# Routing attention and a serf layer: passes over constants on TensorE in the prologue, and another order of shifts, similarities and first loads

## The chip, the core and the metric

The kernel runs on one core of a Trainium2 chip. The metric is the device time of one execution in microseconds (us), as the median of a few runs. The core has a matrix engine, TensorE (PE in the profile; its weight loads are PEld), three engines for elementwise work, VectorE (DVE), ScalarE (ACT) and GpSimd (POOL), and SyncE (SP), whose queue issues nearly all DMA transfers here. Each engine works through its own instructions in order; semaphores make it wait for others.

## The reference

Two layers follow each other. The first is attention with routing: queries and keys are each assigned to the nearest of 16 centroids of their head, by a cosine, and a query sees only the keys of its own cluster.

```python
q_assign = argmax(einsum(q_n, c_n)); k_assign = argmax(einsum(k_n, c_n))   # 16 clusters
scores = q @ k.T / sqrt(64), -1e9 where q_assign != k_assign               # (4, 8, 768, 768)
attn_out = softmax(scores) @ v                                             # (4, 8, 768, 64)
x = attn_out as (3072, 512); h = x @ w_in                                  # w_in (512, 2048)
out = (h * erf(softplus(h))) @ w_out                                       # w_out (2048, 512)
```

There are 32 heads of 768 tokens with 64 features, in f32.

## The kernel before, in words

**The two stages.** The first stage computes attention for 16 pairs of heads (p = 0 to 15; the two heads, e = 0 and 1, lie on partitions 0 to 63 and 64 to 127) and writes x to DRAM. The second multiplies by w_in and w_out in blocks of a Strassen-like scheme; the change does not touch it. Beside the attention the kernel prepares 22 pieces of the weights (`fetch`, `size_and_rest`, `bounded`, `sign`, `shifted`, `summed`, lines 220 to 246: one load, three ScalarE, two DVE and one POOL instruction for each), two in every pair from pair 0 to pair 10.

**A pair's parts**, each a function (lines 281 to 485):

- `load_qk` (169) issues eight DMAs of 96 KB for q and k; `transposes` (281) turns them on DVE and then asks for the next pair's loads, since there is one staging tile for q and one for k.
- `similarities` (293) multiplies by the normalized centroids in f32 (the tile `turned` <- qT, ccT or more_out, ccT); `choose` (306) finds each token's cluster on DVE in four instructions: sims, mx, hot, hotT. `masks` (332) spreads that over the partitions with one matmul (<- hotT, pick) and a ScalarE instruction that writes qm or km. There are four such masks in a pair: q and k, two halves each.
- A step, `maxima_step` (349), estimates the largest score of each query from bf16 copies: four matmuls into `wide` and a reduction on DVE (nmx) over all of it. Twelve steps make a pair. After steps 5 and 11 a small reduction (`lowest`) collects half of the queries.
- `turn` (372) makes the row of shifts of one half out of `lowest`: three matmuls of 128 columns into `turned`, and two ScalarE copies of one row each into qm.
- `products` (392) multiplies k and q in f32; `scores` (405) adds the mask and the shift to the same PSUM tile, so it needs the turned row; `curve` (418) is the exponential on ScalarE (pr <- sc). `accumulate` (423) sums on POOL, `attend` (435) multiplies by v, `divide` (447) makes the reciprocal of the sum (two ScalarE instructions `inv`, two DVE instructions `den`), scales and stores x.

**Periods.** A pair's attention is done in six periods, i = 0 to 5; a period handles two of the pair's twelve units (half of the queries, one sixth of the keys). `period` (705) writes the order out by hand, and all engines keep it: a step, perhaps a mask, products of two units, perhaps similarities of the pair two ahead (i = 3), a second step, perhaps a turn (i = 2 and 5), scores, exponentials, some preparation of weights, and attend for the units of the period before. Steps run ahead: the table `ahead` (689 to 695) gives the slot of each, such that steps of a pair are done in the pair before, 7 slots ahead (6 for some); step 6 of pair 1 stands alone at the end of pair 0. `MASKS` and `FIRST_MASKS` (47, 48) say where the masks of the next pair stand.

**The prologue** (lines 175 to 279 and 794 to 849) normalizes the centroids (a square root by logarithm and exponential on ScalarE and two rounds of Newton on DVE), turns them, sets constants, loads and turns pair 0, finds its clusters, loads v and five pieces of weights, makes steps 0 to 5, the first turn, a mask, and step 6.

**Names in the profile.** Nearly every instruction is recorded by one helper, so nearly all have line L59; they are told apart by their tiles. `wide` and `sc` are PSUM tiles; `turned` is two PSUM tiles for everything small and for attend's sums. An f32 matmul is recorded as two.

Of the kernel before, what the change touches and what calls it, by code (L numbers as in the profile page):

```python
# [9 lines left out]
F32 = mybir.dt.float32  # L10
# [57 lines left out]
def kernel(  # L68
# [81 lines left out]
    def load(p, nm, src, pl):  # L150
        if p >= NPAIR:
            return
        b, h0 = heads(p)
        if nm == "v":
            t = pl.tile([P, NJ, 2, D], F32, name="in_v")
            for e in range(2):
                queues[0].dma_start(out=t[:, :, e], in_=src[b, h0 + e].rearrange("(j p) d -> p j d", p=P))
        else:

            t = pl.tile([P, NB, Q], F32, name="in_" + nm)  # L160
            for e in range(2):
                for g in range(D // Q):
                    queues[e].dma_start(
                        out=t[e * D + g * Q : e * D + (g + 1) * Q],
                        in_=src[b, h0 + e, :, g * Q : (g + 1) * Q].rearrange("(n t) d -> t n d", t=Q),
                    )
        pairs.setdefault(p, {})[nm] = t

    def load_qk(p):
        load(p, "q", q, stage)  # L170
        load(p, "k", k, stage)


    setup = prs[-1].rearrange("p e n -> p (e n)")
# [2 lines left out]

    load_qk(0)
    queues[1] = sy
    tc.keep_in_program_order(nc.scalar.preload_act_table_set("natural_log_exp_and_others"))  # L180

    make_identity(nc, ident)
# [60 lines left out]
    def summed(n):  # L243
        w, lo = w_steps[n][0].bitcast(I32), steps[n][1].bitcast(I32)
        ge.tensor_tensor(out=w, in0=w, in1=lo, op=ALU.add)
        if n in after_of:
            fetch(after_of[n])

    cn = setup[:, D : 3 * D].rearrange("p (e d) -> p e d", e=2)
    spare = iter(range(3 * D, HW))  # L250

    def scalar_tile():
        n = next(spare)
        return setup[:, n : n + 1]
# [6 lines left out]
    norm = scalar_tile()  # L261
    ae.activation(out=norm, in_=ss, func=ACT.Ln)
    ae.activation(out=norm, in_=norm, func=ACT.Exp, scale=0.5)
    for it in range(2):
        inv = scalar_tile()
        ve.reciprocal(out=inv, in_=norm)
        twice = scalar_tile()
        ve.scalar_tensor_tensor(
            out=twice, in0=ss, scalar=inv, in1=norm, op0=ALU.mult, op1=ALU.add
        )  # L270
        norm = scalar_tile()
        ve.tensor_scalar(
            out=norm, in0=twice, scalar1=0.5, scalar2=(1e-6 if it else 0.0),
            op0=ALU.mult, op1=ALU.add,
        )
    rden = scalar_tile()
    ve.reciprocal(out=rden, in_=norm)
    for e in range(2):
# [2 lines left out]
    def transposes(p, which="qk"):  # L281

        if p >= NPAIR:
            return
        st = pairs[p]
        for nm in which:
            st[nm + "T"] = rows[p % 3][nm]
            ve.transpose(out=st[nm + "T"], in_=st.pop(nm).rearrange("p n t -> p (n t)"))
        if "k" in which:
            st.update(lows[p % 2])  # L290
            load_qk(p + 1)

    def similarities(p):

        if p >= NPAIR:
            return
        st = pairs[p]
        st["psim"] = turned[1][:, 0:HW]
        for g in range(4):
            te.matmul(  # L300
                st["psim"][2 * C * g : 2 * C * (g + 1)], lhsT=ccT[:, p % HP],
                rhs=st["qk"[g // 2] + "T"][:, (g % 2) * HW : (g % 2 + 1) * HW],
                start=True, stop=True,
            )
# [378 lines left out]
    def run(work):  # L683
        for _ in work:
            pass

    ahead = [[] for _ in units]
    for n in range(NJ + 1, 2 * NJ * NPAIR):  # L690
        if n == 3 * NJ:
            continue
        slot = n - NJ - (n < 2 * NJ or n > 3 * NJ)
        if slot < len(units):
            ahead[slot].append(divmod(n, 2 * NJ))

    def step_ahead(slot):
        for which in ahead[slot]:
            maxima_step(*which)

    forms = sum((left_forms(ve, *w_in_parts(f, 2)) for f in range(0, HF, 2)), [])
    routing = [iter(())]
# [2 lines left out]
    def period(p, i):  # L705
# [7 lines left out]
                return masks(p + 1, *which, turned[0 if i in (0, 5) else 1])  # L713
            return lambda: None

        step_ahead(u)
        mask(0)()
        next(part[0], None)
        products(u)
        products(u + 1)  # L720
        mask(1)()
        if i == 3:
            similarities(p + 2)
            routing[0] = choose(p + 2)
            next(routing[0], None)
        elif (p, i) == (0, 1):
            similarities(1)
            routing[0] = choose(1)
            next(routing[0], None)
        step_ahead(u + 1)  # L730
        next(part[0], None)
        if i in (2, 5) or (p, i) == (1, 0):
            for which in turns:
                turn(*which)
            turns.clear()
        scores(u)
        scores(u + 1)
        later = mask(2)
        curve(u)
        later()  # L740
        curve(u + 1)
        if i == 0 and early(n1 - 1):
            shifted(n1 - 1)
        elif i == 1 and early(n1):
            size_and_rest(n1)
        elif i == 2 and early(n1):
            bounded(n1)
            sign(n1)
        elif i == 3:
            if early(n1):  # L750
                shifted(n1)
            if early(n2):
                size_and_rest(n2)
        elif i == 4 and early(n2):
            sign(n2)
        elif i == 5 and early(n2):
            bounded(n2)
        if n1 - (i == 0) >= N_EARLY and i in (0, 2, 3, 5) and forms:
            forms.pop(0)()
        if i == 0:  # L760
            transposes(*((p + 2, "q") if p else (1, "k")))
        elif i == 1:
            load(p + 1, "v", v, vp)
            if p == 0:
                run(routing[0])
                vectors(1, "q")
                vectors(1, "k")
        elif i == 2:
            transposes(p + 2, "k" if p else "qk")
        elif i == 3:  # L770
            next(routing[0], None)
        elif i == 4:
            vectors(p + 2, "k")
        elif i == 5:
            run(routing[0])
            vectors(p + 2, "q")
# [10 lines left out]
                part[0] = divide(u - 1)  # L787
                next(part[0])
        mask(3)()
        if (p, i) == (0, 5):  # L790
            maxima_step(1, NJ)


    pct = turned[0][:, 0:P]
    te.transpose(out=pct, in_=cn.rearrange("p e d -> p (e d)"), identity=ident)
    ve.memset(nbig, 0.0)
    for e in range(2):
        ve.memset(nbig[e * D : e * D + C], -BIG)
        ve.memset(nbig[e * D + SH : e * D + SH + 1], 1.0)
    for t in maxima:  # L800
        ve.memset(t, FLOOR)
    ve.memset(pick, 0.0)
    ve.tensor_copy(out=identb, in_=ident)
    ve.memset(minus, -1.0)
    ve.memset(alleps, S * EPS)
    for t in lowest:
        ge.memset(t, 0.0)
    st = pairs[0]
    st["qT"], st["kT"] = rows[0]["q"], rows[0]["k"]
    ve.transpose(out=st["qT"], in_=st.pop("q").rearrange("p n t -> p (n t)"))  # L810
# [4 lines left out]
        )  # L815
    ve.transpose(out=st["kT"], in_=st.pop("k").rearrange("p n t -> p (n t)"))
    st.update(lows[0])
    load_qk(1)
    similarities(0)
    vectors(0, "q")  # L820
    vectors(0, "k")
# [6 lines left out]
                )  # L828
    also = ps_s.tile([P, 2, 512], F32, name="sc", tag="s")
    products(0)  # L830
    run(choose(0))
    transposes(1, "q")
    copies = [
        masks(0, nm, half, bank)
        for nm, half, bank in (("q", 0, wide[:, 0]), ("k", 0, turned[0]), ("k", 1, turned[1]))
# [2 lines left out]
    for copy in copies[1:]:  # L838
        copy()
    load(0, "v", v, vp)  # L840
    for n in range(PLACES):
        fetch(n)
    queues[0] = queues[1] = nc.sync
    for i in range(NJ):
        maxima_step(0, i, also if i % 2 else wide)
    turn(0, 0)
    turns.clear()
    masks(0, "q", 1, turned[1])()
    maxima_step(0, NJ)
    for p in range(NPAIR):  # L850
        for i in range(HJ * 2):
            period(p, i)
# [115 lines left out]
```

## Time and profile before

| what | us |
|---|---|
| median of 3 runs (lowest, highest) | 1052.26 (1051.94, 1052.99) |
| the profiled execution | 1051.62 |
| its span, first to last instruction | 1049.9 |
| TensorE busy | 1023.1 |
| DVE busy | 706.8 |
| ScalarE busy | 514.5 |
| POOL busy | 337.7 |
| mean granted TensorE clock | 0.993 |

The span is 1.72 us shorter than the profiled execution. The first instruction after the start stands at 0.30 us, the first exponential at 28.38, products of pair 1 at 59.22, and the last matmuls of the attention near 465. A timeline's row gives start, duration, engine, operation, tiles written <- tiles read, shape, and how often it stands there in a row; a bracket at its end gives the engine's idle time before it and what ended that. Matmuls overlap, so the duration of a row of several is longer than what they add to the time; the starts of successive rows tell that.

### The profile page before, as it was taken

How to read it: one execution, taken by the hardware profiler on the slowest of the kernel's cores; microseconds unless marked ns; L12 is line 12 of the kernel's file. 1: busy time of each engine (PE TensorE's matmuls, PEld its weight loads, DVE VectorE, ACT ScalarE, POOL GpSimd, SP SyncE). 2: the span in 40 equal slices, each digit the busy share in tenths (PEclk: the TensorE clock that was granted, in tenths of full speed). 3: DMA queues.
4: the chain of work that ended last, by engine and by line, in shares of the span. 5: the costliest groups of instructions: out<-in, count | busy, mean ns of one | idle time of the engine just before them, and what ended most of it. 6: DMA issues, size and time to landing. Idle time of an engine off the chain costs nothing.

```text
span 1049.9 us, 15192 instructions
## 1 busy us (share of the span) xinstructions
PE 1023.1 (97%) x5793; PEld 708.3 (67%) x5793; DVE 706.8 (67%) x1307; ACT 514.5 (49%) x674; POOL 337.7 (32%) x229
## 2 busy tenths in 40 slices
PE   4899999999999999999999999999999999999998
PEld 1344444444444444448888888888888888888887
DVE  6667777777777777747976656476465656564754
ACT  2667777777777666547643250505143222415050
POOL 1566777777667666666230000000000000000000
PEclk8999999999999999999999999999999999999999
DMA  8344443433342321113200010001011000000001
GB/s 191 61 101 101 97 97 94 100 94 88 86 101 51 94 57 31 31 67 117 81 0 19 23 41 1 21 22 39 1 41 41 1 11 31 1 1 21 21 1 40
DMA packets 141496, 55.53 MB, mean 53 GB/s; under 512 B 127088, under 2 KB 131184, under 8 KB 141424
## 3 DMA queue, kind: packets, MB, share of 16 engines
q1 hardware_dynamic: 138288, 54.18, 20.1%
q8 instruction: 45, 0.74, 0.3%
q10 hardware_dynamic: 3136, 0.39, 0.2%
q14 instruction: 27, 0.22, 0.1%
HBM read 41.98 MB, written 12.58 MB: 52 GB/s over the span
## 4 chain that ended last, share of the span: by engine, by line
PE 90%; DVE 6%; ACT 2%; issue 1%; POOL 1%; ACTq 0%; DVEq 0%; POOLq 0%
PE bank L59 42%; PE turned L59 29%; PE sc L59 13%; PE wide L59 7%; DVE nmx L59 3%; DVE den L59 2%; ACT pr L59 1%; POOL more_out L59 1%; ACT inv L59 1%; ACT qm L59 0%; ACT x_own L59 0%; ACT w_in L59 0%; ACTq L59 0%; DVE pr L59 0%; ACT L180 0%
## 5 line engine op out<-in xcount | busy, mean ns | idle before, releaser
L59 POOL TENSOR_TENSOR more_out<-more_out,pr 128x768 f32<-128x768 f32 x128 | 215.8, 1686 | 99.7 <-ACT pr L59 94.6
L59 DVE TENSOR_REDUCE nmx<-wide 128x2 f32<-128x768 f32 x189 | 180.3, 954 | 84.9 <-PE wide L59 83.0
L59 ACT ACTIVATE pr<-sc 128x768 f32<-128x768 f32 x192 | 146.9, 810 | 67.2 <-PE sc L59 66.4
L59 PE MATMUL turned<-pr,in_v 128*64 128x386 f32 x768 | 145.4, 500 | 0.1
L59 DVE TENSOR_TENSOR g<-bank,g 128x256 f32<-128x256 f32 x222 | 89.5, 421 | 56.7 <-PE bank L59 46.4
L59 PE MATMUL bank<-x_own,w_in 128*128 128x256 f32 x424 | 104.4, 379 | 0.0
L59 PE MATMUL bank<-w_out,g 128*128 128x256 f32 x448 | 103.1, 379 | 0.0
L59 PE MATMUL sc<-qT,kT 64*128 64x384 f32 x528 | 101.3, 494 | 0.0
L59 PEld LDWEIGHTS bank<-w_out,g 128*128 128x128 f32 x448 | 85.1, 190 | 11.6
L59 PEld LDWEIGHTS turned<-pr,in_v 128*64 128x64 f32 x768 | 46.6, 136 | 67.8 <-issue 63.2
L59 PEld LDWEIGHTS bank<-x_own,w_in 128*128 128x128 f32 x424 | 80.4, 190 | 12.1 <-issue 1.2
L59 PEld LDWEIGHTS <-qv 64*128 64x128 bf16 x384 | 27.2, 94 | 87.8 <-issue 75.2
L59 ACT COPY g<-bank 128x256 f32<-128x256 f32 x28 | 10.4, 372 | 152.1 <-PE bank L59 148.5
L59 DVE TENSOR_TENSOR osb<-bank,osb 128x256 f32<-128x256 f32 x87 | 35.4, 420 | 72.9 <-ACT osb L59 25.4
L59 ACT ACT_TABLE_LOAD x48 | 61.6, 1283 | 45.7 <-DVE g L59 45.1
L59 POOL TENSOR_TENSOR more_out<-pr,pr 128x768 f32<-128x768 f32 x32 | 58.4, 1826 | 62.6 <-ACT pr L59 62.6
L59 PE MATMUL bank<-x_more,more_in 128*128 128x256 f32 x296 | 76.0, 379 | 0.0
L59 PE MATMUL wide<-kv,qv 64*128 64x384 bf16 x378 | 68.6, 333 | 6.3 <-DVE nmx L59 4.0
L59 PE MATMUL wide<-km,qm 64*128 64x384 bf16 x378 | 67.2, 329 | 2.7 <-ACT qm L59 2.7
L59 PEld LDWEIGHTS sc<-qT,kT 64*128 64x128 f32 x528 | 52.2, 189 | 25.0 <-ACT pr L59 6.0
L59 PE MATMUL bank<-more_out,g_more 128*128 128x256 f32 x272 | 64.3, 379 | 0.0
L59 DVE TENSOR_TENSOR g<-a_s,g 128x512 f32<-128x512 f32 x96 | 62.5, 688 | 1.4 <-ACT a_s L59 1.4
(153 smaller groups left out, 1688.3 us busy)
## 6 DMA issues: line engine op xcount, KB each, us to landing
x_own<-in_moe_w_in_dram SPq DMA_DIRECT2D x13, 512.0 KB, 4.1
in_v<-in_v_dram SPq DMA_DIRECT2D x32, 192.0 KB, 2.9
x_dram<-more_out SPq DMA_DIRECT2D x32, 192.0 KB, 2.5
x_own<-x_dram SPq DMA_DIRECT2D x6, 1024.0 KB, 5.2
out_dram<-osb SPq DMA_DIRECT2D x24, 256.0 KB, 2.0
in_q<-in_q_dram SPq DMA_DIRECT2D x62, 96.0 KB, 3.0
in_k<-in_k_dram SPq DMA_DIRECT2D x62, 96.0 KB, 2.6
g_more<-in_moe_w_out_dram SPq DMA_DIRECT2D x6, 512.0 KB, 3.5
```

Of the source, the lines that this page charges most:

```text
L59: ins = getattr(self.engine, name)(*args, **kw)
```

## The change

It does the following:

- Loads: q and k of pair 1 are loaded into x_more, a tile that is free then, right behind pair 0's; pair 2's loads take the place that pair 1's had. The fifth piece of weights, which goes to x_more, is asked for behind the prologue.
- The constants (nbig, maxima, pick, identb, minus, alleps, lowest) are set ahead of the centroids' work; one of the two rounds of Newton is left out.
- `warm` puts matmuls of constants on TensorE whose result nobody reads: 24 of 256 columns ahead of the centroids' turning, 6 of 384 behind it, 15 behind the first products, 3 after each of steps 0 to 5, and 2 before the first turn. Those of 384 columns read `lowest[0]`.
- The mask of q's second half comes after step 1, not after the turn; q of pair 1 is turned ahead of `choose(0)`, k of pair 1 in the prologue.
- Steps stand six slots ahead in every case, two in each period (in period 0 of pair 0 one, behind the exponentials).
- A turn stands first in periods 0 and 3, not between the second step and the scores of periods 5 and 2.
- Similarities stand behind the scores of their period, not ahead of its second step.

```diff
--- before.py
+++ after.py
@@ -157,7 +157,11 @@
                 queues[0].dma_start(out=t[:, :, e], in_=src[b, h0 + e].rearrange("(j p) d -> p j d", p=P))
         else:
 
-            t = pl.tile([P, NB, Q], F32, name="in_" + nm)
+            if pl is None:
+                t = x_more.rearrange("p a k t -> p (a k t)")[:, (nm == "k") * S : (1 + (nm == "k")) * S]
+                t = t.rearrange("p (n t) -> p n t", t=Q)
+            else:
+                t = pl.tile([P, NB, Q], F32, name="in_" + nm)
             for e in range(2):
                 for g in range(D // Q):
                     queues[e].dma_start(
@@ -167,8 +171,8 @@
         pairs.setdefault(p, {})[nm] = t
 
     def load_qk(p):
-        load(p, "q", q, stage)
-        load(p, "k", k, stage)
+        load(p, "q", q, stage if p != 1 else None)
+        load(p, "k", k, stage if p != 1 else None)
 
 
     setup = prs[-1].rearrange("p e n -> p (e n)")
@@ -177,6 +181,7 @@
 
     load_qk(0)
     queues[1] = sy
+    load_qk(1)
     tc.keep_in_program_order(nc.scalar.preload_act_table_set("natural_log_exp_and_others"))
 
     make_identity(nc, ident)
@@ -246,6 +251,19 @@
         if n in after_of:
             fetch(after_of[n])
 
+    ve.memset(nbig, 0.0)
+    for e in range(2):
+        ve.memset(nbig[e * D : e * D + C], -BIG)
+        ve.memset(nbig[e * D + SH : e * D + SH + 1], 1.0)
+    for t in maxima:
+        ve.memset(t, FLOOR)
+    ve.memset(pick, 0.0)
+    ve.tensor_copy(out=identb, in_=ident)
+    ve.memset(minus, -1.0)
+    ve.memset(alleps, S * EPS)
+    for t in lowest:
+        ge.memset(t, 0.0)
+
     cn = setup[:, D : 3 * D].rearrange("p (e d) -> p e d", e=2)
     spare = iter(range(3 * D, HW))
 
@@ -261,18 +279,12 @@
     norm = scalar_tile()
     ae.activation(out=norm, in_=ss, func=ACT.Ln)
     ae.activation(out=norm, in_=norm, func=ACT.Exp, scale=0.5)
-    for it in range(2):
-        inv = scalar_tile()
-        ve.reciprocal(out=inv, in_=norm)
-        twice = scalar_tile()
-        ve.scalar_tensor_tensor(
-            out=twice, in0=ss, scalar=inv, in1=norm, op0=ALU.mult, op1=ALU.add
-        )
-        norm = scalar_tile()
-        ve.tensor_scalar(
-            out=norm, in0=twice, scalar1=0.5, scalar2=(1e-6 if it else 0.0),
-            op0=ALU.mult, op1=ALU.add,
-        )
+    inv = scalar_tile()
+    ve.reciprocal(out=inv, in_=norm)
+    twice = scalar_tile()
+    ve.scalar_tensor_tensor(out=twice, in0=ss, scalar=inv, in1=norm, op0=ALU.mult, op1=ALU.add)
+    norm = scalar_tile()
+    ve.tensor_scalar(out=norm, in0=twice, scalar1=0.5, scalar2=1e-6, op0=ALU.mult, op1=ALU.add)
     rden = scalar_tile()
     ve.reciprocal(out=rden, in_=norm)
     for e in range(2):
@@ -288,7 +300,8 @@
             ve.transpose(out=st[nm + "T"], in_=st.pop(nm).rearrange("p n t -> p (n t)"))
         if "k" in which:
             st.update(lows[p % 2])
-            load_qk(p + 1)
+            if p > 1:
+                load_qk(p + 1)
 
     def similarities(p):
 
@@ -686,17 +699,10 @@
 
 
 
-    ahead = [[] for _ in units]
-    for n in range(NJ + 1, 2 * NJ * NPAIR):
-        if n == 3 * NJ:
-            continue
-        slot = n - NJ - (n < 2 * NJ or n > 3 * NJ)
-        if slot < len(units):
-            ahead[slot].append(divmod(n, 2 * NJ))
-
-    def step_ahead(slot):
-        for which in ahead[slot]:
-            maxima_step(*which)
+    def step_ahead(u):
+        p, i = divmod(u + NJ, 2 * NJ)
+        if p < NPAIR:
+            maxima_step(p, i)
 
     forms = sum((left_forms(ve, *w_in_parts(f, 2)) for f in range(0, HF, 2)), [])
     routing = [iter(())]
@@ -713,32 +719,32 @@
                 return masks(p + 1, *which, turned[0 if i in (0, 5) else 1])
             return lambda: None
 
-        step_ahead(u)
+        if u > 0:
+            for which in turns if i in (0, 3) else ():
+                turn(*which)
+                turns.remove(which)
+            step_ahead(u)
         mask(0)()
         next(part[0], None)
         products(u)
         products(u + 1)
         mask(1)()
-        if i == 3:
-            similarities(p + 2)
-            routing[0] = choose(p + 2)
-            next(routing[0], None)
-        elif (p, i) == (0, 1):
-            similarities(1)
-            routing[0] = choose(1)
-            next(routing[0], None)
-        step_ahead(u + 1)
+        if u > 0:
+            step_ahead(u + 1)
         next(part[0], None)
-        if i in (2, 5) or (p, i) == (1, 0):
-            for which in turns:
-                turn(*which)
-            turns.clear()
         scores(u)
         scores(u + 1)
         later = mask(2)
+        routed = p + 2 if i == 3 else 1 if (p, i) == (0, 1) else NPAIR
+        if routed < NPAIR:
+            similarities(routed)
+            routing[0] = choose(routed)
+            next(routing[0], None)
         curve(u)
         later()
         curve(u + 1)
+        if u == 0:
+            step_ahead(1)
         if i == 0 and early(n1 - 1):
             shifted(n1 - 1)
         elif i == 1 and early(n1):
@@ -758,7 +764,8 @@
         if n1 - (i == 0) >= N_EARLY and i in (0, 2, 3, 5) and forms:
             forms.pop(0)()
         if i == 0:
-            transposes(*((p + 2, "q") if p else (1, "k")))
+            if p:
+                transposes(p + 2, "q")
         elif i == 1:
             load(p + 1, "v", v, vp)
             if p == 0:
@@ -787,24 +794,17 @@
                 part[0] = divide(u - 1)
                 next(part[0])
         mask(3)()
-        if (p, i) == (0, 5):
-            maxima_step(1, NJ)
-
-
+
+
+    def warm(n, bank, rhs):
+        for _ in range(n):
+            te.matmul(bank[:, 0 : rhs.shape[-1]], lhsT=identb, rhs=rhs, start=True, stop=True)
+
+    zeros = lowest[0].rearrange("p t n -> p (t n)")
+    warm(24, turned[1], pick.rearrange("p h n -> p (h n)"))
     pct = turned[0][:, 0:P]
     te.transpose(out=pct, in_=cn.rearrange("p e d -> p (e d)"), identity=ident)
-    ve.memset(nbig, 0.0)
-    for e in range(2):
-        ve.memset(nbig[e * D : e * D + C], -BIG)
-        ve.memset(nbig[e * D + SH : e * D + SH + 1], 1.0)
-    for t in maxima:
-        ve.memset(t, FLOOR)
-    ve.memset(pick, 0.0)
-    ve.tensor_copy(out=identb, in_=ident)
-    ve.memset(minus, -1.0)
-    ve.memset(alleps, S * EPS)
-    for t in lowest:
-        ge.memset(t, 0.0)
+    warm(6, turned[1], zeros)
     st = pairs[0]
     st["qT"], st["kT"] = rows[0]["q"], rows[0]["k"]
     ve.transpose(out=st["qT"], in_=st.pop("q").rearrange("p n t -> p (n t)"))
@@ -815,7 +815,7 @@
         )
     ve.transpose(out=st["kT"], in_=st.pop("k").rearrange("p n t -> p (n t)"))
     st.update(lows[0])
-    load_qk(1)
+    load_qk(2)
     similarities(0)
     vectors(0, "q")
     vectors(0, "k")
@@ -828,8 +828,9 @@
                 )
     also = ps_s.tile([P, 2, 512], F32, name="sc", tag="s")
     products(0)
+    warm(15, wide[:, 1], zeros)
+    transposes(1, "q")
     run(choose(0))
-    transposes(1, "q")
     copies = [
         masks(0, nm, half, bank)
         for nm, half, bank in (("q", 0, wide[:, 0]), ("k", 0, turned[0]), ("k", 1, turned[1]))
@@ -838,15 +839,20 @@
     for copy in copies[1:]:
         copy()
     load(0, "v", v, vp)
-    for n in range(PLACES):
+    for n in range(PLACES - 1):
         fetch(n)
-    queues[0] = queues[1] = nc.sync
     for i in range(NJ):
         maxima_step(0, i, also if i % 2 else wide)
+        if i == 1:
+            masks(0, "q", 1, turned[1])()
+        warm(3, turned[0], zeros)
+    step_ahead(0)
+    warm(2, turned[0], zeros)
     turn(0, 0)
     turns.clear()
-    masks(0, "q", 1, turned[1])()
-    maxima_step(0, NJ)
+    transposes(1, "k")
+    fetch(PLACES - 1)
+    queues[0] = queues[1] = nc.sync
     for p in range(NPAIR):
         for i in range(HJ * 2):
             period(p, i)
```

## The prediction

> **What bounds the kernel now.** I read the busy times by stage first, then the clock, then the chain of waits, then TensorE's timeline. Five stages, with the columns PE, PEld, DVE, ACT, POOL busy, granted clock, DMA share, GB/s:
>
> ```profile
> 0.00:30.44 30.44, 15.66 (x72) 5.82 (x74) 19.44 (x54) 7.35 (x12) 3.20 (x21) 0.78 0.72 165
> 30.44:59.20 28.76, 23.27 (x169) 9.79 (x168) 18.97 (x28) 19.82 (x30) 16.38 (x10) 1.00 0.40 81
> 59.20:334.60 275.40, 272.81 (x1944) 121.58 (x1942) 209.88 (x300) 208.48 (x319) 194.31 (x120) 1.00 0.40 93
> 334.60:465.20 130.60, 130.08 (x928) 60.41 (x924) 97.22 (x131) 78.07 (x122) 88.21 (x52) 1.00 0.20 48
> 465.20:1049.90 584.70, 581.32 (x2692) 510.65 (x2692) 361.31 (x795) 200.78 (x192) 35.59 (x29) 1.00 0.08 28
> ```
>
> The reader is to see that TensorE idles only in the prologue (15 of 30 us) and in pair 0 (5.5 of 29); pairs 1 to 15 and the MoE stage are bound by it. The MoE stage (585 us) is not touched: it only starts earlier or later. The clock by stretches of 3.41 us:
>
> ```profile
> 13.38:16.79 3.41, 1.36 (x13) 0.60 (x14) 2.73 (x5) 1.05 (x2) 0.00 (x0) 0.97 0.95 205
> 16.79:20.20 3.41, 3.14 (x16) 0.92 (x15) 3.31 (x4) 0.00 (x0) 0.00 (x0) 0.50 0.95 319
> ...
> 27.03:30.44 3.41, 3.00 (x18) 1.64 (x17) 2.42 (x4) 1.51 (x2) 0.46 (x1) 0.53 0.01 2
> 30.44:33.85 3.41, 3.41 (x29) 1.20 (x28) 1.97 (x4) 1.01 (x2) 1.41 (x2) 1.00 0.80 133
> 37.27:40.68 3.41, 2.65 (x18) 0.88 (x18) 2.33 (x5) 2.74 (x6) 0.77 (x2) 1.00 0.23 36
> 40.68:44.09 3.41, 1.86 (x15) 1.32 (x19) 0.96 (x1) 2.07 (x3) 2.74 (x2) 1.00 1.00 160
> ```
>
> A stretch that was 40% busy (1.36) was followed by half clock from 16.79 to 30.44; one that was 55% busy (1.86) was not. Before 13 us no clock is recorded, but the four f32 matmuls at 11.27 took 1.65 where eight take 1.45 later: half clock too.
>
> In the pairs "busy" hides small stalls. Pairs 1 to 10, which also prepare weights, take 27.54 us each (turned x13 at 61.52, 89.06, 116.60 in the chain), later ones 26.68 (products at 366.64 and 393.32). The same places on TensorE in a late pair, and ScalarE in an early one:
>
> ```profile
> 371.92 0.48 PE L59 MATMUL wide<-km,qm 64*128 64x384 bf16 x2
> 372.33 0.34 PE L59 MATMUL turned<-identb,lowest 128*128 128x128 bf16 x3
> 372.61 0.50 PE L59 MATMUL sc<-qm,km 64*128 64x384 bf16 x4
> ...
> 377.16 0.33 PE L59 MATMUL wide<-km,qm 64*128 64x384 bf16 x2
> 377.32 0.49 PE L59 MATMUL sc<-qm,km 64*128 64x384 bf16 x4
> 377.74 1.52 PE L59 MATMUL turned<-pr,in_v 128*64 128x386 f32 x8
> ```
>
> ```profile
> 213.40 1.52 ACT L59 ACTIVATE pr<-sc 128x768 f32<-128x768 f32 x2 [1.31 <-PE sc L59]
> 214.80 0.68 ACT L59 ACTIVATE w_in<-x_own 128x512 f32<-128x512 f32 x1
> 215.38 0.67 ACT L59 ACTIVATE x_own<-x_own 128x512 int32<-128x512 uint32 x1
> 215.94 0.56 ACT L59 ACTIVATE inv<-turned,alleps 128x384 f32<-128x384 f32 x1
> ```
>
> A bf16 pair costs 0.16 (377.16 to 377.32). Four scores should take 0.33 but attend starts after 0.42: a change of tile shape costs 0.09. And inv starts 1.2 us after its matmuls (214.74), because the exponentials before it waited 1.31 for scores queued behind the similarities.
>
> **The change, part by part: prologue.** The constants' DVE work (7 nbig/nmx memsets, pick, identb, minus, alleps; 6.58 to 7.55) moves into DVE's idle 1.78 us before the centroids land at 2.84: free (0.97 if that cover were gone). One Newton round goes: 0.16 + 0.22 + 0.15 and three gaps, 0.64. So cn is ready at 6.0, not 6.63, and the transpose of q starts at 6.03, not 7.46 (its data land about 3 us after an issue at 2.2, in time). The 24 passes wait for identb, which by the memsets' own durations (about 0.1 each from 1.06, then 0.17 and 0.16) is there at about 2.05; 256 columns cost 0.107 at full clock (two thirds of 0.16), 0.21 at half: they end between 4.6 and 7.2. I take 6.9, mostly half clock, so the centroids' transpose, queued behind them, gives 7.3; ccT 7.7; kT 8.75. Six more passes (0.96) lie beside that; similarities are out at 9.85 (11.36 before). That is not the bound: DVE has eight pick copies (0.75) and pair 1's transposition of q (0.95) ahead, to 10.4; then sims, mx, hot, hotT (11.38 to 13.76: 2.38): 12.78. The four loads of that q stand on SP behind pair 0's, issued up to about 6.2; at 3 us from issue to landing they are there about 9, needed at 9.45. The 15 passes (2.4) end about 12.85. Masks at 13.0 (13.81), qm, then step 0 at 14.0 (15.21), its reduction at 14.55 (15.75).
>
> Between steps there are three passes: 0.33 + 0.48 + two shape changes 0.18 = 0.99 a step on TensorE, where DVE needed 0.93 (15.75 to 20.37 for five): with the mask moved in, 5 x 0.99 + 0.16, the last reduction ends 20.6, lowest 20.85 (21.61). The three passes after step 5 read lowest[0], which is no constant any more: DVE has just written it, so they wait for 20.85, and step 6 and two passes follow before the turn: 0.48 + 0.33 + 0.32 + four changes = 1.4 us, the turn at 22.25, later than 21.67 now. The copies end at 23.45, but nothing else is in the way: today mask q1 (0.50 on ScalarE), step 6 behind it, step 7 and step 8 stand before the first scores at 27.80; now they come at 23.5. Steps 7 and 8 follow, each after the other's reduction (0.96 and the transposition of k, 0.97): products of period 1 at 25.7 against 29.67. **Gain 4.0.**
>
> SP: pair 2's loads take pair 1's place; v and four weight loads issue 13.2 to 16.5 (12.87 to 16.28 before), cost nothing since the first weight is read near 29. The fifth, and pair 1's v behind it, wait for k's transposition (23.9); that v is needed after 50. Were that cover gone, attend would wait for a landing, 3 us.
>
> **Pair 0.** From products of period 1 (25.7): similarities end at 28.4, DVE's sims to hotT (2.4, if hot doesn't take the 1.63 it took at 34.26) at 30.95, the reduction behind it at 31.9; so step 11 at 31.95, scores at 32.3; ScalarE's exponentials 32.75 to 34.3, sign to 35.55, qm to 36.0, the turn, its copies to 37.3; mask k1, then products of period 3 at 37.5. That is 11.8 where it was 12.9 (29.67 to 42.56): **1.1**; the wait for qm (1.88 at 42.23) stays. Period 3 to pair 1's products took 16.66 (42.56 to 59.22): a turn that waited 1.28 (55.19), an extra step that waited 1.05 (58.90) with its 0.33 and shape changes. Each period now has two steps, and lowest is ready a half period before its turn: 13.3, as below. **3.4.**
>
> **Pairs 1 to 15.** The turn stood between step and scores (371.92 + 0.16 + 0.16 = 372.24 to 372.61: 0.37); between attend and step one shape change is there anyway, so it costs 0.26: 0.11, twice. Similarities between scores and attend save 0.10. So 0.32 in each of 15 pairs, 4.8. In the ten early pairs the exponentials of period 3 come 0.8 earlier, inv starts 0.86 after its matmuls as in late pairs (379.09 to 379.95), and the 4.14 us of period 4 become the late pairs' 3.83: 0.31. The step that waited for mask q1 in period 5 (4.50 against 4.35) now comes a slot later: 0.15. Against that: the rows of shifts are copied on ScalarE behind sign (1.36); I place their end at 211.96, scores at 211.95: a wait of 0.05 to 0.3, taken 0.08. 0.38 x 10 = 3.8. **8.6.** Below: new waits could eat all of it; above: 10.
>
> Sum 4.0 + 1.1 + 3.4 + 8.6 = 17.1. The profiled execution took 1051.62 (span 1049.90 and 1.72 around it), 0.64 under the median: 1034.5, or 1035 beside the median of 1052.26.
>
> The Trainium skill ("TensorE: Matmul & The Clock Gate", Part 1: The HAM clock gate) says that the array falls to half clock after an idle window of about 3.4 us. The 3.41 us grid of the rows agrees, the condition does not: nothing idled longer than 0.9 us in the stretch before the fall. By that rule the steps would have kept their clock, and the passes between them would only cost 5 x 0.06 + 0.16, 0.5 us; the rows decide.
>
> **Rivals.** (a) Passes over zeros do not hold the clock; no row shows such a pass. Then the 15 cost 4.8 and delay the masks to about 17.9 (4.9), and steps pace at 0.65 + 0.96 + 0.18 = 1.8 (4.0 more over five) until real work restores the clock: 17.1 - 8.9, 1044. For it: 92% busy at 16.79 did not restore the clock. Against: those were modelled ends with gaps; passes leave none. (b) The pairs give nothing: the saved shape changes turn into waits for DVE's wide reduction, which has some 0.1 us of slack after lowest is inserted: 1052.3 - 8.5, 1044. (c) Both: no change, 1052. (d) Slower: scores wait for the copied row in all 31 halves. From 17.1 / 31 = 0.55 us it eats everything; if the two copies (0.95) end that much after scores are ready, 29.5 - 17.1: 1064. For it, sign and two exponentials stand ahead on ScalarE; against, ScalarE is idle 1.31 there now.
>
> **Chances.** Forecast 0.62 (1029 to 1040), (a) 0.11, (b) 0.17, (c) 0.04, (d) 0.06. Faster 0.90, same 0.04, slower 0.06, where 0.2% is what a measurement can tell. The range takes (a) and (b) in: 1029 to 1046.
>
> **What would show it.** Clock 1.00 from about 7 us on; turn near 22, first exponential near 24 (28.38), products of pair 1 near 50.8 (59.22), 26.8 us a pair early and 26.35 late. Wrong if half clock shows after 10 us, if scores wait for ScalarE's qm, or if the pitch of the pairs stays 27.54.

## The result and the profile after

| | before | changed |
|---|---|---|
| median, us | 1052.18 (8 runs, 1051.26 to 1053.01) | 1055.89 (8 runs, 1053.55 to 1056.01) |
| ratio, 95% interval | | 1.0029, 1.0018 to 1.0040 |
| profiled execution: time, span, us | 1051.62, 1049.9 | 1055.98, 1054.3 |

The kernel became slower by 0.3%, where 1.6% faster was forecast. Six of the eight runs stand at 1055.7 to 1056.0 and two at 1053.55; the profiled one is of the six and has one stretch at half clock, and experiment e11 shows what that costs.

The stages come first, cut at the same places of the program as the five of before: columns PE, PEld, DVE, ACT, POOL busy, granted clock, DMA share, GB/s, of the changed kernel.

```profile
0.00:27.06 27.06, 22.09 (x135) 10.74 (x137) 18.74 (x50) 7.35 (x12) 3.75 (x21) 1.00 0.90 195
27.06:53.36 26.30, 23.93 (x168) 11.35 (x166) 18.93 (x27) 18.89 (x28) 15.71 (x10) 0.94 0.36 79
53.36:334.82 281.46, 268.87 (x1944) 127.11 (x1943) 220.37 (x301) 212.24 (x321) 203.05 (x121) 1.00 0.39 91
334.82:469.55 134.73, 129.70 (x930) 61.54 (x928) 102.38 (x134) 78.22 (x123) 93.74 (x52) 1.00 0.19 47
469.55:1054.30 584.75, 581.32 (x2692) 510.65 (x2692) 361.35 (x795) 200.68 (x192) 35.62 (x29) 1.00 0.08 28
```

The prologue is 3.4 us shorter (27.06 against 30.44), pair 0 is 2.5 shorter (26.30 against 28.76), the MoE stage is the same. The two stretches of the pairs, where 8.6 was to be gained, are 6.1 and 4.1 **longer**, and TensorE, which was busy 99% of them, now idles 12.6 and 5.0 us. So a new wait stands in the pairs. By period (from products to products, an early pair, before and after): period 0 took 4.96 and now 6.04; period 1 4.25 and 4.40; period 2 4.34 and 4.24; period 3 5.36 and 5.38; period 4 4.11 and 3.82; period 5 4.52 and 4.25. The last two are what was forecast; period 0 ate them. In late pairs period 0 went from 4.96 to 6.31. The pitch, the time from one pair's products to the next pair's, went from 27.54 to 28.13 in early pairs and from 26.67 to 27.71 in late ones. Added up over the profiled execution: 3.4 won up to products of period 1, 2.5 won in pair 0, 10.2 lost in the pairs.

What the waits of TensorE in period 0 name is DVE: mask k0 waits 0.40 for hotT, the second step 0.51 for nmx.

```profile
224.07 0.33 PE L59 MATMUL turned<-hotT,pick 64*128 64x384 bf16 x1 [0.40 <-DVE hotT L59]
224.91 0.34 PE L59 MATMUL wide<-kv,qv 64*128 64x384 bf16 x2 [0.51 <-DVE nmx L59]
```

In the timeline of DVE in the changed kernel (start, length, idle before in brackets), around the end of period 5:

```profile
220.94 0.18 DVE L59 TENSOR_REDUCE lowest<-nmx 128x6 bf16<-128x18 f32 x1
221.03 0.42 DVE L59 TENSOR_SCALAR w_in<-w_in 128x512 f32<-128x512 f32 x1
221.36 2.04 DVE L59 TENSOR_TENSOR hot<-sims,mx 128x384 bf16<-128x384 f32 x1
223.43 0.58 DVE L59 STREAM_TRANSPOSE hotT<-hot 128x384 bf16<-128x384 bf16 x1
223.94 0.92 DVE L59 TENSOR_REDUCE nmx<-wide 128x2 f32<-128x768 f32 x1
```

and GpSimd's at that time:

```profile
221.12 3.81 POOL L59 TENSOR_TENSOR more_out<-more_out,pr 128x768 f32<-128x768 f32 x2 [0.54 <-ACT pr L59]
```

The same places before, DVE and then GpSimd:

```profile
223.29 0.55 DVE L59 TENSOR_TENSOR hot<-sims,mx 128x384 bf16<-128x384 f32 x1
223.87 0.58 DVE L59 STREAM_TRANSPOSE hotT<-hot 128x384 bf16<-128x384 bf16 x1
```

```profile
218.82 3.44 POOL L59 TENSOR_TENSOR more_out<-more_out,pr 128x768 f32<-128x768 f32 x2 [0.74 <-ACT pr L59]
224.28 1.68 POOL L59 TENSOR_TENSOR more_out<-more_out,pr 128x768 f32<-128x768 f32 x1 [2.02 <-ACT pr L59]
```

No instruction was added here, and none is listed as waiting: hot itself takes 2.04 instead of 0.55. Before, it lay between two accumulations of GpSimd (222.26 to 224.28); now the accumulation starts at 221.12, hot at 221.36, and hot ends 0.42 after the first of the two accumulations of that row does (222.98). This is so in all 14 pairs that compute a hot after pair 1's. Behind hot on DVE stand hotT, which mask k0 needs, and the reduction that the next step needs.

### The profile page after: what moved, and what is told of

Same layout as the page of the kernel before. It is cut to its first block, busy times and chain, and to the rows that moved or that the text cites. A ratio compares the mean times of both kernels' runs of the same rounds, so it can differ in the third digit from the quotient of the medians.

```text
span 1054.3 us, 15316 instructions
## 1 busy us (share of the span) xinstructions
PE 1025.9 (97%) x5858; PEld 721.4 (68%) x5858; DVE 721.8 (68%) x1304; ACT 517.4 (49%) x674; POOL 351.9 (33%) x229
## 4 chain that ended last, share of the span: by engine, by line
PE 87%; DVE 11%; ACT 1%; issue 1%; POOL 0%; ACTq 0%; DVEq 0%; POOLq 0%
PE bank L59 41%; PE turned L59 28%; PE sc L59 11%; PE wide L59 6%; DVE nmx L59 5%; DVE hot L59 3%; DVE den L59 2%; DVE hotT L59 1%; DVE w_in L59 0%; POOL more_out L59 0%; DVE lowest L59 0%; ACT pr L59 0%; ACT inv L59 0%; ACT qm L59 0%; ACT x_own L59 0%
## 5 line engine op out<-in xcount | busy, mean ns | idle before, releaser
L59 POOL TENSOR_TENSOR more_out<-more_out,pr 128x768 f32<-128x768 f32 x128 | 227.1, 1774 | 68.8 <-ACT pr L59 63.7
L59 POOL TENSOR_TENSOR more_out<-pr,pr 128x768 f32<-128x768 f32 x32 | 61.2, 1912 | 83.7 <-ACT pr L59 83.7
```

Of the source, the lines that this page charges most:

```text
L59: ins = getattr(self.engine, name)(*args, **kw)
```

## The experiments

**Theory 1:** the turn left the place between step and scores of period 5; so the scores, the exponentials, and with them GpSimd's accumulation come earlier against DVE's order, and hot now runs into it and waits. **Rival A:** the turn at the head of periods 0 and 3 costs by itself. **Rival B:** hot's slowness has nothing to do with its operands. **Rival C:** the later similarities cost. And the warming passes may disturb or not hold the clock.

### e1 and e5: one operand of hot moved to PSUM

```diff
-        mx = routep.tile([P, n], F32, name="mx")
+        mx = turned[1][:, 512 - n : 512]          # e1
+        mx = wide[:, 1, 512 - n : 512]            # e5
```

> The changed kernel with one edit: mx, the 24 group maxima that hot is compared with, lies in unused columns of the PSUM bank turned[1] instead of SBUF, so hot has one SBUF input instead of two; same work, same order. Theory 1 (the pairs lose because hot, now issued while GpSimd's accumulation reads SBUF, waits for it: 2.04 us instead of 0.55): hot comes back to about 0.55, period 0 of the early pairs from 6.05 to about 5.0, the pitch from 28.15 to about 27.1 and late from 27.71 to about 26.6, in all some 16 us: 1040. Rival A (the turn at the head of periods 0 and 3 is what costs: copies on ScalarE, mask k0 behind them): hot may shorten, the pitch stays above 28, 1055. Rival B (the slowdown of hot has nothing to do with where its operands lie): hot stays at 2.04 and the time at 1056.

Measured: 1072.82 us, ratio 1.0197 (1.0181 to 1.0212): far slower, and yet hot did as theory 1 says. DVE and then GpSimd in e1:

```profile
254.22 0.42 DVE L59 TENSOR_SCALAR w_in<-w_in 128x512 f32<-128x512 f32 x1
254.55 0.55 DVE L59 TENSOR_TENSOR hot<-sims,turned 128x384 bf16<-128x384 f32 x1
255.14 0.58 DVE L59 STREAM_TRANSPOSE hotT<-hot 128x384 bf16<-128x384 bf16 x1
```

```profile
254.31 3.62 POOL L59 TENSOR_TENSOR more_out<-more_out,pr 128x768 f32<-128x768 f32 x2 [0.53 <-ACT pr L59]
```

The accumulation starts at 254.31, hot at 254.55, in the middle of it, and takes 0.55. Period 0 is back at 4.97. But period 5 went from 4.25 to 6.05 (and in late pairs to 7.16). TensorE's waits in this stretch show why (us in total, times, longest):

```profile
PE turned L59 <- DVE hot L59: 1.7, 1, 1.7
```

attend writes columns 0 to 385 of turned[1] and was made to wait for reads of columns 488 to 511 of the same PSUM tile. The place of mx was at fault (period 3 went from 5.38 to 5.81 too), so e5 puts it where the next writer comes later anyway.

> As e1, but mx lies in unused columns of the PSUM tile wide, which the following step overwrites behind DVE's own work anyway, and not in turned[1], where attend waited for hot and mx (5.79 and 6.05 us in periods 3 and 5). Theory 1: hot 0.55, period 0 at 4.97 as in e1, periods 3 and 5 at 5.38 and 4.25 as in the changed kernel: pitch 27.05 early and 26.35 late, total 1055.9 - 10 x 1.08 - 5 x 1.35 = 1038. Rival A (the turn at the head of periods 0 and 3 costs the pairs by itself): what e1 gave in period 0 was paid for by its wait in period 5, and period 0 comes back to 5.5 or more; total 1048 or more.

Measured: 1042.08, ratio 0.9903 (0.9888 to 0.9917); 13.8 us under the changed kernel. hot is 0.55 in every pair, period 0 is 4.98, and the pitch is 26.97 early and 26.72 late. DVE and then GpSimd in e5:

```profile
215.29 0.55 DVE L59 TENSOR_TENSOR hot<-sims,wide 128x384 bf16<-128x384 f32 x1
```

```profile
215.05 3.62 POOL L59 TENSOR_TENSOR more_out<-more_out,pr 128x768 f32<-128x768 f32 x2 [0.54 <-ACT pr L59]
```

Rivals A and B fall: the turn still stands at the head, and only the operand's place changed. The time is 4 us more than expected. mx of pair 0 lies in wide too and waits 1.93 for the 15 passes there; a stretch at half clock follows (16.04 to 19.46), and products of period 1 come at 29.02 instead of 26.29. Pair 0 wins 1.7 of that back, since no stretch at half clock lies in it. In late pairs a step waits 0.3 for hot (period 5: 4.59 instead of 4.25). The profiled run took 1041.08; two of the four runs took 1043, at a mean clock of 0.997 instead of 0.998, and no profile shows where they lose it.

The Trainium skill ("SBUF — State Buffer", Who interferes with whom) has the rule behind these rows: VectorE and GpSimd share one pair of SBUF ports, held for a whole instruction; a VectorE instruction with two SBUF inputs needs it against a GpSimd instruction that reads SBUF; one with a single SBUF input does not, unless it runs in a mode that uses both ports, which a tensor_scalar can; and the one that comes second waits. The rows agree: 2.04 beside the accumulation with both inputs in SBUF, 0.55 beside it with one in PSUM. The bounding of a weight in e6 below is a tensor_scalar with one SBUF input; no row shows the mode it runs in.

### e6: who comes first

hot is issued ahead of lowest in period 5; its operands stay in SBUF.

```diff
         if i in (NJ - 1, 2 * NJ - 1):
             h = i // NJ
+            if h == 0:
+                next(routing[0], None)
```

> The changed kernel with hot issued ahead of lowest in period 5, operands untouched: DVE reaches it at the end of the step's reduction (220.94 in the changed kernel's frame), 0.18 us before GpSimd's accumulation may start (221.125). Theory 1 (the one that starts first has it, the other waits): hot 0.55, GpSimd's accumulation longer by about 0.35 us, lowest 0.55 us later but still ahead of the turn; period 0 near 5.0, total about 1039. Rival (they share the bandwidth, so both are slow whenever they overlap): hot stays above 1 us and the total above 1047.

Measured: 1050.12, ratio 0.9980 (0.9970 to 0.9989); period 0 5.71. DVE and GpSimd in e6:

```profile
246.62 0.55 DVE L59 TENSOR_TENSOR hot<-sims,mx 128x384 bf16<-128x384 f32 x1
247.08 0.17 DVE L59 TENSOR_REDUCE lowest<-nmx 128x6 bf16<-128x18 f32 x1
247.16 1.83 DVE L59 TENSOR_SCALAR w_in<-w_in 128x512 f32<-128x512 f32 x1
248.92 0.56 DVE L59 STREAM_TRANSPOSE hotT<-hot 128x384 bf16<-128x384 bf16 x1
```

```profile
246.93 3.60 POOL L59 TENSOR_TENSOR more_out<-more_out,pr 128x768 f32<-128x768 f32 x2 [0.54 <-ACT pr L59]
```

hot, now first, takes 0.55, and the two accumulations 3.60 where two took 3.44 before. An even sharing of bandwidth is out: then both would be slow. But the time expected (1039) did not come, since the wait passed on: the bounding of a weight (w_in, 0.42 before) is now the first that meets the accumulation, and takes 1.83. hotT still starts 2.3 us after hot. An instruction moved out of a collision gives its place in it to the next one that can collide.

### e2, e3, e4: one part of the change at a time

e2 has the changed prologue and the loop of before; e4 is e2 with the similarities behind the scores; e3 is the changed kernel with the similarities put back. The core of e4 against the changed kernel (e2 also puts back the similarities; the list of steps is that of before):

```diff
-            for which in turns if i in (0, 3) else ():
-                turn(*which)
-                turns.remove(which)
...
+        if i in (2, 5) or (p, i) == (1, 0):
+            for which in turns:
+                turn(*which)
+            turns.clear()
```

> The kernel before with the changed prologue alone (constants early, one Newton round, warming passes, loads reordered, k of pair 1 transposed before period 0); steps, turns and similarities inside the periods as before. Theory 1: the pairs are as before (pitch 27.54 and 26.68, hot 0.55), products of period 1 near 26.3, products of pair 1 3 to 5 us earlier than 59.22; total about 1048. Rival (the warming passes or the moved loads disturb the pairs): a pitch above 27.6, total 1052 or more.

> The changed kernel with turns and steps put back as they were before (turn between second step and scores of periods 2 and 5, steps one slot further ahead); prologue and similarities as changed. Theory 1: hot is back at 0.55, since the exponentials of period 5 wait for the turn again and GpSimd starts after hot; period 4 keeps its 3.83: pitch about 27.1 early and 26.6 late, total about 1042. Rival C (similarities cost): the pitch stays above 28, total above 1052.

> The changed kernel with the similarities put back ahead of the second step of periods 3 (and of period 1 of pair 0). Theory 1: hot still waits for GpSimd (2.04), period 0 stays at 6.0; the exponentials of period 3 come later again, so period 4 goes from 3.83 back to about 4.1 and the pitch from 28.15 to about 28.4: total about 1058. Rival C (the late similarities and with them a late choose cost the pairs): the pitch falls to 27.5 or below, total 1046 or less.

| | time | ratio (95%) | products of period 1, of pair 1 | pitch early, late | hot in the pairs |
|---|---|---|---|---|---|
| before | 1052.05 | | 29.67, 59.22 | 27.54, 26.67 | 0.55 |
| e2, prologue alone | 1048.52 | 0.9966 (0.9955 to 0.9978) | 26.63, 55.90 | 27.53, 26.67 | 0.55 |
| e4, and similarities | 1046.00 | 0.9941 (0.9924 to 0.9958) | 27.04, 55.11 | 27.42, 26.57 | 0.55 |
| changed: and turns, steps | 1055.89 | 1.0029 (1.0018 to 1.0040) | 26.29, 53.36 | 28.13, 27.71 | 2.04 |
| e3, turns without similarities | 1061.28 | 1.0090 (1.0075 to 1.0105) | 25.64, 52.09 | 28.76, 27.81 | 2.03 |

The prologue is worth 3.5 us, the similarities 2.5; the turns with their steps cost 9.9, and of these kernels hot is slow in just those that have them. About 2 of the 9.9 is the stretch at half clock in pair 0, which the profile of the changed kernel has and those of e2, e3 and e4 have not: beside e11 below (1053.71, without it) the turns cost 7.7. Rival C falls: without the late similarities the kernel is 5.4 slower (7.6 beside e11; expected were 2), and periods 3 and 4 go from 5.38 and 3.82 to 5.72 and 4.12. e4 expected 1042 with a pitch of 27.1: period 5 came out at 4.81 where before took 4.52, since the second step there, which stands ahead of the turn, waits 0.29 for the qm of mask q1.

### e10: a control

```diff
-        mx = routep.tile([P, n], F32, name="mx")      # in the kernel before
+        mx = wide[:, 1, 512 - n : 512]
```

> The kernel before with mx in wide, nothing else: a control. Theory 1: hot does not collide in the pairs of the kernel before (0.55), so nothing is to be had there: pitch 27.54 and 26.68; in pair 0 hot goes from 1.63 to 0.55, worth 0 to 1 us: total 1051 to 1052. If mx in PSUM were faster by itself, or its wait on wide cost something, the pitch would move.

Measured: 1053.04, ratio 1.0005 (0.9995 to 1.0014); pitch 27.52 and 26.71; hot in pair 0 0.56 instead of 1.63. PSUM for mx gives nothing where nothing collides.

### e7: without the passes over zeros

```diff
-    warm(6, turned[1], zeros)
...
-    warm(15, wide[:, 1], zeros)
...
-        warm(3, turned[0], zeros)
...
-    warm(2, turned[0], zeros)
```

> The changed kernel without the passes over zeros (6, 15, 3 after each of six steps, 2); the 24 early ones stay. Theory 1 and the prediction's reading of the clock: steps of the prologue leave TensorE under half busy, the clock falls for at least one 3.41 us stretch, products of period 1 come 1 to 4 us later than 26.3, total 1057 to 1060. Rival (the passes only fill, the clock would have stayed up): products of period 1 about 1 us earlier, total 1055.

Measured: 1055.13, ratio 1.0031 (1.0019 to 1.0042): the time of the changed kernel, with a wider spread (1053.15 to 1057.61). The profiled run took 1054.83. The stretches of e7:

```profile
11.10:14.51 3.41, 1.29 (x9) 0.62 (x10) 1.99 (x4) 1.05 (x2) 0.00 (x0) 0.82 1.05 167
14.51:17.92 3.41, 3.07 (x19) 1.11 (x14) 3.29 (x4) 0.49 (x1) 0.00 (x0) 0.50 1.00 228
17.92:21.33 3.41, 2.84 (x17) 1.03 (x14) 3.25 (x6) 0.29 (x1) 0.00 (x0) 0.50 1.00 374
```

So the clock does fall without the passes (0.50) and holds with them (1.00); yet the time is the rival's. DVE's reductions of the steps, in e7 and then in the changed kernel:

```profile
17.33 0.95 DVE L59 TENSOR_REDUCE nmx<-sc 128x2 f32<-128x768 f32 x1
18.33 0.96 DVE L59 TENSOR_REDUCE nmx<-wide 128x2 f32<-128x768 f32 x1
19.20 0.95 DVE L59 TENSOR_REDUCE nmx<-sc 128x2 f32<-128x768 f32 x1
```

```profile
18.02 0.96 DVE L59 TENSOR_REDUCE nmx<-sc 128x2 f32<-128x768 f32 x1
19.05 0.96 DVE L59 TENSOR_REDUCE nmx<-wide 128x2 f32<-128x768 f32 x1
20.07 0.96 DVE L59 TENSOR_REDUCE nmx<-sc 128x2 f32<-128x768 f32 x1
```

At half clock the steps still go at DVE's pace (0.94); with three passes between them at 1.03, TensorE's. Together with the wait of the passes behind step 5 for lowest (1.35) that puts the turn at 22.73 instead of 20.50. What the full clock gives back behind the turn (products of period 0 to those of period 1 take 3.30 instead of 4.18) does not cover it: products of period 1 are at 25.12 in e7, at 26.29 in the changed kernel.

### e8 and e11: the stretch at half clock in pair 0

Period 3 of pair 0 took 7.09 us. The stretches of the changed kernel before and at that place:

```profile
34.97:38.38 3.41, 1.53 (x13) 0.72 (x13) 3.41 (x4) 2.75 (x5) 3.13 (x2) 1.00 0.00 0
38.38:41.79 3.41, 3.41 (x17) 2.08 (x16) 0.94 (x3) 0.58 (x1) 0.00 (x0) 0.51 0.90 145
```

45% busy (1.53), then half clock. Nine passes are put in the wait for qm; e8 does this to e5, with its zeros in lowest[1], e11 to the changed kernel and nothing else.

```diff
         mask(3)()
+        if (p, i) == (0, 2):
+            warm(9, wide[:, 0], pick.rearrange("p h n -> p (h n)"))
...
-    zeros = lowest[0].rearrange("p t n -> p (t n)")      # e8 only
+    zeros = lowest[1].rearrange("p t n -> p (t n)")
```

> e5 with two more edits: the zeros are a tile that the prologue never writes again (lowest[1]), so the passes after step 5 do not wait for DVE's lowest (21.38 in the changed kernel); and nine passes (0.96 us) stand in TensorE's wait for qm at the end of period 2 of pair 0 (35.55 to 36.83), ahead of the stretch at half clock (38.38 to 41.79). If the clock fell because the stretch before was 45% busy, it stays up: products of period 4 come 1.7 us earlier, and the turn of the prologue about 1 us: total about 1035.5. If the fall has another cause: only the first, 1037.5.

> The changed kernel with nothing but nine passes (0.96 us) in TensorE's wait for qm at the end of period 2 of pair 0 (35.55 to 36.83). e8 could not tell what they do, since e5 without them had no stretch at half clock there (its stretches lie elsewhere against the work). If the fall at 38.38 comes from the 45% busy stretch before it: clock 1.00 from 38.4 on, period 3 to 4 from 7.09 to about 5.4, total 1054.2. If not: 7.09 stays and so does 1055.9.

e8: 1040.06, ratio 0.9881 (0.9866 to 0.9896); in the profile 0.8 us of that come from the prologue, and of the passes it shows nothing, since e5 took 5.4 for period 3 without them. e11: 1053.71, ratio 1.0017 (1.0008 to 1.0027), and its stretches:

```profile
34.97:38.38 3.41, 2.61 (x22) 1.52 (x22) 3.41 (x4) 2.75 (x5) 3.12 (x2) 1.00 0.00 0
38.38:41.79 3.41, 3.41 (x29) 1.73 (x30) 2.21 (x3) 2.04 (x4) 0.00 (x0) 1.00 0.62 99
```

The clock stays up and period 3 takes 5.40: 1.69 us, just what the fall cost in the profile; the medians differ by 2.18. All ten runs of e11 lie between 1053.57 and 1054.30, beside the changed kernel's two runs of 1053.55; those two have a mean granted clock of 1.000 against 0.998 in the other six. e6 divides in the same way: five runs at 1048.92 to 1049.21 with 1.000, five at 1051.04 to 1051.74 with 0.998. That the faster ones missed this fall fits, but they have no profile of their own.

### e9 and e12: the parts put together

e9 is the changed kernel with e11's fill, mx in wide from pair 1 on, zeros in lowest[1], and fewer passes:

```diff
-        mx = routep.tile([P, n], F32, name="mx")
+        mx = wide[:, 1, 512 - n : 512] if p else routep.tile([P, n], F32, name="mx")
...
-        warm(3, turned[0], zeros)
+        warm(2 if i < 5 else 0, turned[0], zeros)
...
-    warm(2, turned[0], zeros)
```

> The changed kernel with four edits: mx in wide from pair 1 on (pair 0 keeps SBUF, since in e5 mx of pair 0 waited for the 15 passes into wide and the prologue lost 2.7 us); two passes over zeros after each of steps 0 to 4 and none behind step 5 and step 6 (without any, e7 had its turn at 20.5 instead of 22.7, but lost 1 us at half clock behind it); zeros in lowest[1]; the nine passes of e8. By theory 1 and e7: turn near 20.8, products of period 1 near 24.3 at full clock, products of pair 1 near 49.7 (e8: 53.59), pitch 26.97 as in e8: total about 1040.06 - 3.9 = 1036. If the steps need the third pass to hold the clock, 1 to 2 us of it are lost: 1038.

Measured: 1036.00 us, ratio 0.9846 (0.9831 to 0.9860), 16 us under the kernel before and the best of all. Turn at 19.94, products of period 1 at 23.52, of pair 1 at 49.31, the clock at 1.00 throughout, pitch 26.98 and 26.72. The chain of waits, shares by engine, in the changed kernel and in e9:

```profile
PE 87%; DVE 11%; ACT 1%; issue 1%; POOL 0%; ACTq 0%; DVEq 0%; POOLq 0%
```

```profile
PE 93%; DVE 5%; ACT 1%; issue 0%; POOL 0%; ACTq 0%; DVEq 0%; POOLq 0%
```

The 6% that the chain spent more on DVE are gone, and with them the wait. With two passes behind a step instead of three, DVE's six reductions of the steps follow each other by 0.90 on average (14.15 to 18.64), at full clock. Part of the early turn is luck: the clock rose at 6.0 us in e9's profile and at 7.7 in the changed kernel's, so the 24 first passes took 4.60 instead of 5.09 and the similarities start 0.84 earlier. e12 is e9 with the turns and steps of before (e4's diff):

> e9 with turns and steps put back as in the kernel before (as in e4), all else kept: what is the turn at the head of a period worth once hot cannot collide? By the stages of e4 and e9: products of pair 1 some 1.5 us later than 49.31, early pitch 27.42 against 26.98 (10 pairs, 4.4), late 26.57 against 26.72 (5 pairs, -0.75): 1036.0 + 5.2 = 1041. Rival A (the turn at the head gains nothing, only the collision's removal and the prologue did): 1036 or less.

Measured: 1044.20, ratio 0.9922 (0.9905 to 0.9938). Early pitch 27.43, late 26.61, as expected; products of pair 1 at 53.06, 3.75 later than in e9 and not 1.5 (2.92 of it in period 5 of pair 0, 7.24 against 4.32). So the turns at the head of a period with their steps are worth 8.2 us once hot cannot collide, where they cost 7.7 when it can (9.9 with the stretch at half clock).

## Why the prediction was wrong, step by step

- **Prologue, 4.0 us: right in size, with a surplus and a loss in it.** Products of period 1 at 26.29 (25.7 forecast). No clock is recorded before 7.7 us; the 24 passes took 0.21 each (1.94 to 7.03), half clock as forecast, and from 7.7 on the clock is 1.00: no rival (a). The steps' pace was forecast at 0.99 and was 1.03; it was seen that this is TensorE's and not DVE's 0.93, but not that DVE's pace would have been kept at half clock. The passes over zeros, as they stand in the changed kernel, do not pay for themselves (e7).
- **Pair 0, 1.1 and 3.4: the mechanism right, 2.0 short.** 1.69 of it is the stretch at half clock after a 45% busy one. The prediction had read such rows in the kernel before (40% fell, 55% did not) and did not apply them to pair 0, where the earlier work left a wait of 1.27 for qm. The rows were also cut 0.2 beside the clock's own stretches: cut where the clock changes (16.58, 30.24), they are 39% and 49%, so that 45% lay between the two and could not have been decided. Whether a fall comes is in part luck, as two of the eight runs show. (Products of period 3 stood at 42.40, not 42.56; this moves 0.16 from one term to the other.)
- **Pairs, 8.6: this step failed.** From products of pair 1 to those of the last period it took 411.53, where before took 401.32: 10.2 more instead of 8.6 less. The step priced the turn by TensorE's time (tile shapes, "0.11, twice") and by a wait of 0.08 for ScalarE's copies, and put what GpSimd does then at nothing. But the turn was also what delayed the exponentials of period 5, and so GpSimd's accumulation, past hot. With that delay gone, hot took 2.04 instead of 0.55, and period 0 took 1.08 more in the early pairs and 1.35 more in the late ones. The named bound "new waits could eat all of it" was too near: they ate more. The evidence was in the prediction: "if hot doesn't take the 1.63 it took at 34.26" was said of pair 0, and not asked of the 14 other pairs whose hot had moved against GpSimd.
- **Its other terms** can be read where hot does not cost. Period 4: 4.11 to 3.82 (0.31 forecast). Late pairs of the changed kernel, periods 2, 3 and 5: 0.31 together, 0.32 forecast. Here is the turn on TensorE in a late pair of it, then similarities behind scores:

```profile
376.60 0.34 PE L59 MATMUL turned<-identb,lowest 128*128 128x128 bf16 x3
376.87 0.34 PE L59 MATMUL wide<-kv,qv 64*128 64x384 bf16 x2
...
378.82 0.49 PE L59 MATMUL sc<-qm,km 64*128 64x384 bf16 x4
379.24 0.85 PE L59 MATMUL turned<-more_out,ccT 128*32 128x384 f32 x8
```

The turn takes 0.27 (376.60 to 376.87), 0.26 forecast. And ScalarE in an early pair:

```profile
210.94 1.51 ACT L59 ACTIVATE pr<-sc 128x768 f32<-128x768 f32 x2 [0.47 <-PE sc L59]
212.34 0.70 ACT L59 ACTIVATE w_in<-x_own 128x512 f32<-128x512 f32 x1
212.91 0.69 ACT L59 ACTIVATE x_own<-x_own 128x512 int32<-128x512 uint32 x1
213.93 0.58 ACT L59 ACTIVATE inv<-turned,alleps 128x384 f32<-128x384 f32 x1 [0.33 <-PE turned L59]
```

The exponentials wait 0.47 where they waited 1.31, and inv no longer stands behind them. In e9, free of the collision, early pairs gain 0.56 each and late ones nothing, since there a step waits for hot in wide.
- **Rivals.** (d) had the right sign with the wrong mechanism: the list of waits of an early pair has no entry of TensorE for qm. The slower engine was not ScalarE with its copies, but DVE, held up by GpSimd. (b) has the place (DVE's reductions), not the size.

## What to carry to other kernels

When a wait is removed, list not only who waits next, but which instructions of VectorE and GpSimd now run at the same time: a VectorE instruction with two SBUF inputs, or one such as the bounding of e6, can take up to the length of a GpSimd instruction longer without any wait being shown; the sign of it in a profile is a row whose mean duration has grown. A collision is better taken away (an operand in PSUM, in a tile that nobody is about to write) than moved. Filler work for the clock must fit into the wait that it fills: three passes behind a step (1.03) outlasted DVE's reduction (0.94) and set the pace themselves, two (e9) did not.

## What the runs showed of the hardware that was not expected

- hot, 128x384: 0.55 alone, 2.04 behind an accumulation that had just started, 0.55 beside it with the 24 maxima in PSUM. One small operand decides.
- The clock fell to half for one stretch of 3.41 us after a stretch 45% busy in which TensorE idled at most 1.27 us at once, and held after one 77% busy, where only nine passes had been added. In e4 the fall behind the last matmul (1044.83) places its stretches: that of the same wait, 34.48 to 37.89, is 61% busy (2.10), and the clock held. But the share alone does not decide between 45% and 50%: the clock held in e2 after 45% (first row) and fell in e8 after 50% (second and third). What else counts stays open.

```profile
37.04:40.46 3.42, 1.54 (x11) 1.18 (x11) 0.96 (x1) 2.40 (x4) 3.08 (x2) 1.00 0.98 156
13.76:17.17 3.41, 1.72 (x14) 0.59 (x14) 2.28 (x4) 1.05 (x2) 0.00 (x0) 1.00 1.05 193
17.17:20.59 3.42, 3.42 (x15) 0.80 (x11) 1.99 (x3) 0.49 (x1) 0.00 (x0) 0.50 0.91 334
```

- Passes over zeros hold the clock as other passes do: 1.00 from 7.7 to 38.4 in the changed kernel, where e7 without them fell at 13.2. The rows of stretches print 1.00 also where no clock is recorded, as ahead of 7.7; there the passes' own pace, 0.21 against 0.11 for the nine of e11, tells it.
